# Hashed attention and a two-layer block on one core: other issuers for weight and v loads, engine copies for batch 0's half stacks, a revised planner, and other PSUM tiles for the last output block

## The chip, the cores and the metric

The kernel runs on one core of one Trainium2 chip. The core has a matrix engine (TensorE, PE in the profile, with PEld for its weight loads), a vector engine (VectorE, DVE), a scalar engine (ScalarE, ACT), a general engine (GpSimd, POOL) and a synchronising engine (SyncE, SP) that here only issues DMA transfers. Each engine runs its own instructions strictly in the order in which they stand and waits on semaphores for the others. The metric is the device time of one execution in microseconds (us); less is better.

## The reference

For each of 4 batches and 8 heads, queries and keys get a 6-bit bucket from the signs of a projection; a query sees only the keys of its bucket. Softmax of the scaled scores, times v, gives `attn_out`. Its rows then pass through two matrix products with a squared ReLU between them.

```python
q_bits = (np.einsum('bhsd,dk->bhsk', q, proj) > 0).astype(np.int64)
k_bits = (np.einsum('bhsd,dk->bhsk', k, proj) > 0).astype(np.int64)
mask = q_bucket[:, :, :, None] == k_bucket[:, :, None, :]
scores = np.where(mask, scale * np.matmul(q, k.transpose(0, 1, 3, 2)), -1000000000.0)
...
x = np.ascontiguousarray(attn_out.transpose(0, 2, 1, 3)).reshape(B * S, H * D)
h = np.maximum(x @ w_in, 0.0)
return (h * h @ w_out).astype(np.float32)
```

Sizes: sequence 768, head dimension 64, 3072 tokens, model width 512, hidden width 2048. Everything is float32.

## The kernel before

**Tiling.** The attention is cut into 32 visits: one pair of heads and one half of the sequence (384 queries) each. A visit has six units (three blocks of 128 queries for each head). A unit makes scores of 128 x 768 in PSUM (`pS`, or `pS2` under the name `po` for some early units), VectorE copies them to `e` with the row minimum of the negated scores, ScalarE takes the exponential and its sum, GpSimd or VectorE adds 1e-9 (`rv`), VectorE takes the reciprocal. In the first four visits (`PLAIN_AV`, line 54) GpSimd multiplies `e` by `rv`, TensorE transposes it in float32 (`pT`) and ScalarE or VectorE copies the result to `aT`. In the other 28 visits `e` becomes two fp16 parts (`hl`), which a DMA transposes. `av` then multiplies with v into `pA`, and `xx` takes the result as two fp16 parts.

**Half stacks.** For each head `prep` (lines 631 to 662) loads `R`, 64 rows of transposed keys over 64 rows of transposed queries, splits it into fp16 `A` and the remainder `L`, and builds with five copies of 64 x 768 the operands (`Q`, `A`) and (`M`, `L`) of two score matmuls. The five copies (lines 650 to 652, 659, 660) are DMAs from SBUF to SBUF. Visit 0 is loaded in another form (`first`).

**Weights.** `fetch` (lines 548 to 557) loads 512 columns of raw float64-packed weights (`raw`, three buffers under the tag `hl`); ScalarE or VectorE makes `top`, VectorE makes `f`, then `f` is split into an fp16 high part and the remainder (`win`, `wo`). There are 16 such pieces of w_in and 16 of w_out, nearly all needed early.

**The two-layer block.** When the four head pairs of a batch and half are done, `moe` (lines 807 to 880) runs: for each of 16 slices of the hidden width 12 matmuls into `pm`, ReLU (`g32`), square, split to two fp16 parts `g`, and 9 matmuls into `po`, a PSUM tile of three banks, one for each block of 128 tokens. After the last slice each bank is copied to `o` and sent out. There are eight such blocks, called 0 to 7 here; each is spread among the visits that follow.

**What sets the order.** All operations are first recorded, each with its dependences and one or more ways (engine and instruction). `order` (lines 245 to 272) then plans: `forward` (318 to 399) places operations on engines in simulated time by priorities and by the costs of `cost` (195 to 225), `backward` turns the plan into new priorities, and of five rounds the shortest plan is emitted. An operation with several ways goes to the engine where the plan sees it done first. So a number in the planner can move any instruction. `emit` also puts filler matmuls (`idle<-ones`, line 420) where the plan expects TensorE to wait early on. As every instruction is issued in `emit`, the profile gives nearly all of them the line 427 (424 for grouped matmuls); tiles tell them apart. A second copy of the whole program for inputs out of range follows behind a branch and isn't executed; its instructions are not spoken of.

Of the kernel before, what the change touches and what calls it, by code (L numbers as in the profile page):

```python
# [23 lines left out]
P = 128  # L24
# [105 lines left out]
class Program:  # L130
# [24 lines left out]
    @staticmethod  # L155
    def region(view):
        ap, rec = view.ap, view.rec
        size = lambda dims: 1 + sum(st * (n - 1) for st, n in dims)
        if rec.kind == "dram":
            return 0, 1, ap.offset, ap.offset + size(ap.ap), 0, 0, 0  # L160
        p0, f0 = divmod(ap.offset, rec.row)
        if rec.kind == "psum":
            return 0, 1, f0 // 512, 1 + (f0 % rec.row + size(ap.ap[1:]) - 1) // 512, 0, 0, 0

        (step, n), inner = ap.ap[1], size(ap.ap[2:])
        block = (step, f0 % step, f0 % step + inner) if n > 1 and f0 % step + inner <= step else (0, 0, 0)
        return (p0, p0 + ap.ap[0][1], f0, f0 + size(ap.ap[1:])) + block

    def add(self, *ways):


        ways = [w for w in ways if w[0].key != "pool" or not any(isinstance(x, View) and x.rec.kind == "psum" for x in w[2])]
        queue, name, args, kw = ways[0]
        if name == "matmuls":
            used = [(x, n == 0) for a, _ in args for n, x in enumerate(a)]
        else:
            used = [(args[0], True)] + [(x, False) for x in args[1:]] + [(x, k == "accum_out") for k, x in kw.items()]
        used = [(x.rec, w, self.region(x)) for x, w in used if isinstance(x, View)]
        i, deps = len(self.ops), set()
        for rec, w, (p0, p1, f0, f1, fs, g0, g1) in used:  # L180
            if rec.before is not None:
                deps |= rec.before.ops
            for j, w2, (a0, a1, b0, b1, bs, c0, c1) in rec.accesses:
                if (w or w2 or rec.kind == "psum") and a0 < p1 and p0 < a1 and b0 < f1 and f0 < b1 and not (fs and fs == bs and (c1 <= g0 or g1 <= c0)):
                    deps.add(j)
        for rec, w, r in used:
            rec.ops.add(i)
            rec.accesses.append((i, w, r))
        deps.discard(i)
        if self.mark is not None:  # L190
            self.paced.append((i, self.mark))
        self.ops.append(Op([w + (self.cost(w[0].key, *w[1:]), self.port(w[0].key, *w[1:])) for w in ways], deps, self.rank))

    @staticmethod
    def cost(key, name, args, kw):
# [3 lines left out]
        if name == "matmuls":  # L199

            side = {32: 4, 64: 2}.get(size(args[0][0][1]), 1)
            t = sum(size(a[2]) * column.get(a[2].dtype, 1 / 2.4) + 7 for a, _ in args) / side
            return t, t
        kinds = [x.rec.kind if isinstance(x, View) else "" for x in args]
# [7 lines left out]
        if name.startswith("dma"):  # L212
            b = int(np.prod(args[0].shape)) * mybir.dt.size(args[0].dtype)
            inside = name == "dma_start_transpose" or kinds[:2] == ["sb", "sb"]
            busy = 1040 if key == "pool" else (650 if inside else 475) + 50 * (key == "act")
            return busy, b / (TRANSPOSES if name == "dma_start_transpose" else 314)
        if key == "act":
# [3 lines left out]
        else:  # L221
            fast = name in ("tensor_copy", "tensor_scalar") and "psum" not in kinds[:2]
            both = len(args) > 3 and isinstance(args[3], View) and args[3].shape[-1] == 1
            t = 67 + 100 * ("accum_out" in kw) + n / (1.92 if fast else 0.96) + 62 * (ptr and (fast or name == "scalar_tensor_tensor")) + 100 * both
        return t, t
# [9 lines left out]
    def port(key, name, args, kw):  # L235
# [82 lines left out]
    def forward(self, prio, near):  # L318
# [7 lines left out]
        free = dict.fromkeys(keys, 0.0)  # L326
        out, dma, dge, held, kind = [], 0.0, 0.0, 0.0, None

# [10 lines left out]
        while True:  # L339
# [44 lines left out]
            if o.name.startswith("dma"):  # L384
                dge = max(dge, t) + busy if k != "pool" else dge
                busy = dge - t if k != "pool" else busy
                dma = max(dma, t + busy + (650 if k != "pool" else 450))
                if o.name == "dma_start_transpose":
                    o.busy = busy = dma + 467 - t
                dma += done  # L390
                done = dma + 910 - t
            free[k], o.end = t + busy, t + done
# [56 lines left out]
def run(ctx: ExitStack, tc, kq, v, proj2, w_in, w_out, consts, out, flag):  # L449
# [56 lines left out]
    if fast:  # L506
# [124 lines left out]
    def prep(b, hp):  # L631
# [12 lines left out]
        for odd, R in enumerate(Rs):  # L644
# [4 lines left out]
            pr.rank = r0 + STACKS  # L649
            send(f32(Q[T]), f32(A[U]))  # L650
            send(f32(Q[U]), f32(L[U]))
            send(f32(A[U]), f32(A[T]))
            for half in range(2):
# [4 lines left out]
                dve.tensor_scalar(M[:, w], pc, masks[:, 0:1], masks[:, 1:2], ALU.subtract, ALU.max)  # L658
            send(f32(L[U]), f32(M[T]))
            send(f32(M[T]), f32(Q[T]))  # L660
            out.append(((Q, A), (M, L)))
# [57 lines left out]
    def values(b, hp, plain):  # L719
# [3 lines left out]
        if fast:  # L723
            vscales[b] = VS, None
            RV = sb([P, 2, KC, D], F32, "V", tag="VV" if plain else "R")
            send(RV, v[b, hp])
            if plain:
# [79 lines left out]
    def moe(n, b, half):  # L807
# [6 lines left out]
        for f in range(NF + 1):  # L814
# [23 lines left out]
            if f > 0:  # L838
# [4 lines left out]
                if first:  # L843
                    po = ps([P, 3, DM], F32, "po")
                for t in range(3):
                    gh = g[:, 0, t * P : (t + 1) * P]
                    gl = g[:, 1, t * P : (t + 1) * P]
                    pr.rank, pr.mark = RANK_PE, pace()
                    pe.matmul(po[:, t], gh, wo[:, 0, m], start=first, stop=False)
                    pe.matmul(po[:, t], gh, wo[:, 1, m], start=False, stop=False)  # L850
                    pe.matmul(po[:, t], gl, wo[:, 0, m], start=False, stop=last)
                    pr.mark = None
# [5 lines left out]
                for t in range(3):  # L858
                    r0 = b * S + half * HS + t * P
                    if grouped and last:  # L860
                        if m == 3:
                            move(acc[:, t], po[:, t], back)
                        else:
                            dve.scalar_tensor_tensor(acc[:, t], po[:, t], back, acc[:, t], ALU.mult, ALU.add)
# [168 lines left out]
```

## Time and profile before

| | |
|---|---|
| median of 3 runs | 832.73 us (830.81 to 833.39) |
| the profiled execution | 834.86 us, its span 833.1 us |
| PE busy | 794.3 us, 95% |
| ACT busy | 656.6 us, 79% |
| DVE busy | 605.2 us, 73% |
| POOL busy | 72.7 us, 9% |
| DMA | 145.93 MB, mean 175 GB/s |

The span runs from the first to the last recorded event of the execution; 1.76 us lie around it. Busy times are of the whole span. A row of a group of instructions gives the engine, the operation, the tiles (written and read), the shape, the count, then the total busy time in us and the mean of one in ns, then the idle time in front and who ended it. A row of the list in order of time begins with the start and the length in us, and ends with the idle time before it and its releaser, in brackets.

### The profile page before, as it was taken

Reading aid. Unit: us, or ns where it says so; the run is one execution under the profiler, and the core shown is the slowest. Engines: PE = TensorE matmul, PEld = TensorE weight load, DVE = VectorE, ACT = ScalarE, POOL = GpSimd, SP = SyncE. Lnnn points to the kernel's source line nnn. Section 1 sums busy time; section 2 is a strip of 40 time slices with the busy share of each in tenths; the row PEclk is TensorE's granted clock in tenths of the full one; section 3 lists DMA queues with packets and bytes.
Section 4 is the critical chain, followed back from the end, with each engine's and each line's share of the span. In section 5 each row is a group of like instructions: output and inputs, shape, how many; then the busy total and the mean of one; then the engine's idle time right before and its main releaser. Section 6 shows DMA issues by size and latency. Waiting matters only on the chain. (4 is left out here: it accounts for less than half of the span.)

```text
span 833.1 us, 14383 instructions
## 1 busy us (share of the span) xinstructions
PE 794.3 (95%) x5001; PEld 430.0 (52%) x5001; DVE 605.2 (73%) x1200; ACT 656.6 (79%) x1238; POOL 72.7 (9%) x175
## 2 busy tenths in 40 slices
PE   7797799999999999999999999999999999999996
PEld 4354355555555554555555545555555554555553
DVE  6888989998999888898879755888889433611110
ACT  5898999998888989888898856888988997334443
POOL 1255200100000010000000000000002000000000
PEclk9999999999999999999999999999999999999999
DMA  8985979999999999999989866988975889501001
GB/s 258 270 223 181 292 188 179 214 176 195 183 202 196 195 188 213 192 181 219 194 188 186 212 165 140 181 143 148 146 133 99 239 290 304 212 1 39 1 1 42
DMA packets 299521, 145.93 MB, mean 175 GB/s; under 512 B 268752, under 2 KB 279344, under 8 KB 299440
## 3 DMA queue, kind: packets, MB, share of 16 engines
q1 hardware_dynamic: 299440, 144.93, 77.2%
q8 instruction: 41, 0.67, 0.3%
q14 instruction: 40, 0.33, 0.1%
HBM read 56.80 MB, written 6.29 MB: 76 GB/s over the span
## 5 line engine op out<-in xcount | busy, mean ns | idle before, releaser
L427 PE MATMUL po<-wo,g 128*128 128x512 f16 x1152 | 296.9, 379 | 5.7 <-ACT o L427 5.7
L427 PE MATMUL pm<-xx,win 128*128 128x384 f16 x1536 | 297.7, 326 | 4.4 <-ACT g L427 2.8
L427 PEld LDWEIGHTS <-win 128*128 128x128 f16 x1536 | 149.9, 98 | 116.6 <-issue 8.0
L427 DVE TENSOR_SCALAR_CACHE_REDUCE e<-pS 128x768 f32<-128x768 f32 x192 | 182.7, 953 | 21.9 <-PE pS L427 17.7
L427 ACT ACTIVATE e<-e,maxes 128x768 f32<-128x768 f32 x192 | 178.2, 929 | 20.7 <-DVE e L427 19.2
L427 DVE SCALAR_TENSOR_TENSOR hl<-e,rv,hl 128x768 f16<-128x768 f32 x168 | 171.0, 1019 | 18.8 <-ACT hl L427 17.8
L427 PEld LDWEIGHTS <-g 128*128 128x128 f16 x1152 | 111.9, 98 | 124.8 <-issue 9.1
L427 ACT ACTIVATE hl<-e,rv 128x768 f16<-128x768 f32 x168 | 154.6, 923 | 6.0 <-DMA aT<-hl 5.2
L427 DVE SCALAR_TENSOR_TENSOR g<-g,g 128x384 f16<-128x384 f32 x121 | 66.9, 553 | 111.8 <-ACT g L427 111.4
L427 ACT ACTIVATE g<-g 128x384 f32<-128x384 f32 (+1 forms) x251 | 129.4, 517 | 6.6 <-PE po L427 2.7
L427 ACT ACTIVATE g<-pm 128x384 f32<-128x384 f32 x127 | 61.2, 482 | 90.3 <-PE pm L427 90.0
L427 PE MATMUL pS<-A,Q 128*128 128x384 f16 x372 | 93.1, 330 | 4.1 <-DVE e L427 2.6
L427 PE MATMUL pS<-L,M 128*128 128x384 f16 x372 | 91.8, 327 | 0.8 <-DMA M<-Q 0.8
L424 PE MATMUL pA<-aT,VV 128*64 128x384 f16 x1008 | 87.2, 327 | 0.0
L427 POOL TENSOR_SCALAR rv<-sums 128x1 f32<-128x1 f32 x136 | 36.8, 271 | 541.7 <-ACT e L427 400.2
L424 PEld LDWEIGHTS <-VV 128*64 128x64 f16 x1008 | 54.7, 110 | 32.9 <-issue 10.0
L427 PEld LDWEIGHTS <-Q 128*128 128x128 f16 x372 | 34.2, 98 | 43.1 <-issue 16.2
L427 DVE TENSOR_SCALAR M<-pc,masks 128x384 f16<-128x384 f32 x64 | 43.0, 672 | 15.4 <-PE pc L427 15.2
L427 PEld LDWEIGHTS <-M 128*128 128x128 f16 x372 | 36.3, 98 | 25.1 <-DMA M<-Q 1.2
L427 ACT ACTIVATION_READ_ACCUMULATOR e<-e,maxes 128x1 f32 x192 | 36.6, 191 | 0.0
L427 DVE SCALAR_TENSOR_TENSOR L<-R,A 128x768 f16<-128x768 f32 x32 | 30.4, 950 | 7.7 <-ACT A L427 7.5
L427 PE MATMUL pT<-unit_f,e 128*128 128x128 f32 x144 | 23.8, 293 | 10.5 <-ACT aT L427 7.7
(82 smaller groups left out, 517.4 us busy)
## 6 DMA issues: line engine op xcount, KB each, us to landing
R<-kq SPq DMA_DIRECT2D x32, 384.0 KB, 3.8
X<-kq SPq DMA_DIRECT2D x32, 384.0 KB, 4.1
raw<-w_in SPq DMA_DIRECT2D x16, 511.8 KB, 5.6
raw<-w_out SPq DMA_DIRECT2D x16, 511.8 KB, 4.9
V<-vp SPq DMA_DIRECT2D x20, 384.0 KB, 5.1
out<-o SPq DMA_DIRECT2D x24, 256.0 KB, 2.7
X<-vp SPq DMA_DIRECT2D x16, 384.0 KB, 4.4
Q<-L SPq DMA_DIRECT2D x32, 96.0 KB, 2.9
```

The costliest lines, as they stand in the source:

```text
L424: ins = q.engine.matmul(*map(real, args), **kw).ins
L427: ins = getattr(q.engine, o.name)(*map(real, o.args), **{k: real(x) for k, x in o.kw.items()}).ins
```

## The change

- `HALVES`: in batch 0 (`HALVES_TO` = 1) each of the five half-stack copies may be done by SP (a DMA), GpSimd or VectorE; elsewhere it stays a DMA.
- `RAW_BY`: from the fourth piece on (`RAW_FROM` = 3) a raw weight piece may be loaded by SP or by GpSimd. `V_BY` holds only SP. In the order that results GpSimd issues no transfer at all: all 32 weight pieces and all 20 loads of v stand on SP, as before.
- The planner: a transfer isn't placed while its queue is more than `AT_MOST` (2000 ns) behind; there are two queue clocks that slow each other; a limit of eight SP transfers in flight (`LANES`); other prices for transfers, for two-byte copies on VectorE and for matmuls of 64 rows in pairs; VectorE operations with two inputs no longer count as using the port that VectorE and GpSimd share; a PSUM tile counts as one region.
- The last two-layer block: instead of the three banks of `po`, its outputs are two banks of a `pS` tile and a `pA` tile, and the copy of the middle one is put on VectorE.
- `codes` shares the buffers of `g32`.

```diff
+RAW_BY, V_BY = ("sp", "pool"), ("sp",)
+HALVES, HALVES_TO = (("sp", "pool", "dve"),) * 5, 1
+AT_MOST, RAW_FROM = 2000, 3
...
-        return inside and (len(ins) == 2 or name in ("tensor_copy", "tensor_scalar"))
+        return inside and name in ("tensor_copy", "tensor_scalar")
...
+            if way[1].startswith("dma") and rings[int(k == "pool")] > t + AT_MOST:
+                heapq.heappush(later[k], (rings[int(k == "pool")] - AT_MOST, i))
+                continue
...
-        send(raw.rearrange("p n t -> p (n t)").bitcast(U16)[:, 0:2047], src.bitcast(U16)[:, 1:2048])
+        pr.add(*[(getattr(pr, x), "dma_start", (raw.rearrange("p n t -> p (n t)").bitcast(U16)[:, 0:2047], src.bitcast(U16)[:, 1:2048]), {}) for x in (RAW_BY if turn[0] >= RAW_FROM else ("sp",))])
...
-            send(f32(Q[T]), f32(A[U]))
-            send(f32(Q[U]), f32(L[U]))
-            send(f32(A[U]), f32(A[T]))
+            by = lambda n: tuple(getattr(pr, x) for x in (HALVES[n] if fast and b < HALVES_TO else ("sp",)))
+            move(f32(Q[T]), f32(A[U]), 1.0, by(0))
+            move(f32(Q[U]), f32(L[U]), 1.0, by(1))
+            move(f32(A[U]), f32(A[T]), 1.0, by(2))
...
-                    po = ps([P, 3, DM], F32, "po")
+                    if fast and n == 2 * B - 1:
+                        po = ps([P, 2, 512], F32, "pS"), ps([P, 512], F32, "pA")
+                        po = [po[0][:, 0], po[0][:, 1], po[1]]
+                    else:
+                        po = ps([P, 3, DM], F32, "po")
+                        po = [po[:, t] for t in range(3)]
...
-                        move(o, po[:, t], back)
+                        move(o, po[t], back, (dve,) if fast and t == 1 else (act, dve, pool))
```

Of the 160 half-stack copies 34 leave SP: 21 stand on VectorE and 13 on GpSimd. The order of nearly everything else moves a little too. Three places follow.

SP, near the program's start, behind the constants and the first three weight pieces (`raw`), before:

```order
L427 DMA V_182<-vp 128x768
L427 DMA Q_189<-L_140 64x768
L427 DMA R_195<-kq 128x768
L427 DMA Q_189<-A_97 64x768
L427 DMA R_216<-kq 128x768
L427 DMA Q_221<-L_191 64x768
L427 DMA Q_221<-A_173 64x768
L427 DMA raw_237<-w_in 128x2047
L427 DMA V_241<-vp 128x768
L427 DMA raw_276<-w_out 128x2047
```

The same place now:

```order
L444 DMA R_208<-kq 128x768
L444 DMA R_234<-kq 128x768
L444 DMA unit_f_248<-consts 128x128
L444 DMA raw_252<-w_in 128x2047
L444 DMA raw_266<-w_out 128x2047
L444 DMA raw_301<-w_out 128x2047
L444 DMA V_330<-vp 128x768
L444 DMA Q_307<-A_148 64x768
L444 DMA V_348<-vp 128x768
```

The copies between the loads are gone but for one, the head loads `R` and the weights come ahead of v, and `unit_f` (the identity of the transposes) comes behind them.

GpSimd, its first work, before (`e<-e,rv` is the normalising of one unit's 128 x 768 exponentials, `rv` its small forerunner):

```order
L427 TENSOR_SCALAR rv_257<-sums_244 128x1
L427 TENSOR_SCALAR e_232<-e_232,rv_257 128x768
L427 TENSOR_SCALAR rv_283<-sums_244 128x1
L427 TENSOR_SCALAR e_246<-e_246,rv_283 128x768
L427 TENSOR_SCALAR rv_338<-sums_244 128x1
```

and now:

```order
L444 TENSOR_SCALAR Q_212<-A_140 64x768
L444 TENSOR_TENSOR win_246<-f_239,win_246 128x512
L444 TENSOR_SCALAR rv_264<-sums_259 128x1
L444 TENSOR_SCALAR e_244<-e_244,rv_264 128x768
L444 TENSOR_SCALAR L_144<-M_232 64x768
L444 TENSOR_SCALAR rv_311<-sums_259 128x1
L444 TENSOR_TENSOR win_246<-f_295,win_246 128x512
L444 TENSOR_SCALAR rv_352<-sums_259 128x1
L444 TENSOR_SCALAR Q_359<-L_345 64x768
L444 TENSOR_SCALAR e_261<-e_261,rv_311 128x768
```

Half-stack copies and remainders of weights now stand among the normalisings.

TensorE, its last matmuls, before (`g` are the two fp16 parts of the hidden slice; the three banks of `po` are filled in turn):

```order
L427 MATMUL po_8985<-wo_460,g_9387 128x512
L427 LDWEIGHTS g_9365
L427 MATMUL po_8985<-wo_460,g_9365 128x512 [waits Activation_49]
L427 LDWEIGHTS g_9387
L427 MATMUL po_8985<-wo_460,g_9387 128x512
L427 LDWEIGHTS g_9387
L427 MATMUL po_8985<-wo_460,g_9387 128x512
L427 LDWEIGHTS g_9387
L427 MATMUL po_8985<-wo_460,g_9387 128x512 [waits Activation_49]
```

and now:

```order
L444 LDWEIGHTS g_9391
L444 MATMUL pA_9021<-wo_451,g_9391 128x512
L444 LDWEIGHTS g_9413
L444 MATMUL pS_9007<-wo_451,g_9413 128x512
L444 LDWEIGHTS g_9391
L444 MATMUL pA_9021<-wo_451,g_9391 128x512
L444 LDWEIGHTS g_9391
L444 MATMUL pA_9021<-wo_451,g_9391 128x512
L444 LDWEIGHTS g_9413
L444 MATMUL pA_9021<-wo_451,g_9413 128x512
```

The two waits for ScalarE (its copies of the first two banks) are gone from TensorE's last matmuls.

ScalarE has no single place; counted in its order, this is what stands ahead of its first ReLU of the two-layer block (`g32<-pm`), where the counts differ:

| ScalarE, ahead of the first `g32<-pm` | before | now |
|---|---|---|
| `A<-R` 128x768 | 7 | 8 |
| `VV<-V` 128x768 | 2 | 3 |
| `aT<-pT` 128x384 | 46 | 48 |
| `bits<-pd` 128x384 | 4 | 5 |
| `e<-e,maxes` 128x768, with its sum | 27 | 28 |
| `top<-raw` 128x512 | 24 | 27 |
| `win<-f` and `wo<-f` 128x512 | 23 | 22 |

On VectorE, ahead of its fourth `xx<-pA`, there are 21 half-stack copies, four `f<-raw` and six small `rv` operations more, and two `L<-R`, two `aT<-pT`, one `A<-R`, one `VV<-V` and six remainders of weights fewer. On GpSimd, ahead of the 24th normalising, there are 13 half-stack copies, eight remainders of weights, two `L<-R` and one `wo<-f` more. On TensorE, ahead of the first `pm`, there are 27 fillers, four small `pd` matmuls and three score matmuls more.

More of the change, by code (lines that the diff above doesn't have):

```diff
@@ L64 @@
 RUN = 18
+LANES = 8
 CONSTS_BY, WIDE = ("sp", "sp", "sp"), 1
@@ L162, in region @@
         if rec.kind == "psum":
-            return 0, 1, f0 // 512, 1 + (f0 % rec.row + size(ap.ap[1:]) - 1) // 512, 0, 0, 0
+            return 0, 1, 0, 1, 0, 0, 0
         (step, n), inner = ap.ap[1], size(ap.ap[2:])
@@ L183, in add @@
             for j, w2, (a0, a1, b0, b1, bs, c0, c1) in rec.accesses:
-                if (w or w2 or rec.kind == "psum") and a0 < p1 and p0 < a1 and b0 < f1 and f0 < b1 and not (fs and fs == bs and (c1 <= g0 or g1 <= c0)):
+                if (w or w2) and a0 < p1 and p0 < a1 and b0 < f1 and f0 < b1 and not (fs and fs == bs and (c1 <= g0 or g1 <= c0)):
                     deps.add(j)
@@ L202, in cost @@
             t = sum(size(a[2]) * column.get(a[2].dtype, 1 / 2.4) + 7 for a, _ in args) / side
+            if args[0][0][1].shape[0] == D and len(args) == 2:
+                t *= 0.5 if args[0][0][2].dtype == F32 else 0.7
             return t, t
@@ L215, in cost @@
             busy = 1040 if key == "pool" else (650 if inside else 475) + 50 * (key == "act")
-            return busy, b / (TRANSPOSES if name == "dma_start_transpose" else 314)
+            return busy, SETUP + b / (TRANSPOSES if name == "dma_start_transpose" else INSIDE if inside else LOADING)
         if key == "act":
@@ L223, in cost @@
             both = len(args) > 3 and isinstance(args[3], View) and args[3].shape[-1] == 1
-            t = 67 + 100 * ("accum_out" in kw) + n / (1.92 if fast else 0.96) + 62 * (ptr and (fast or name == "scalar_tensor_tensor")) + 100 * both
+            t = 67 + 100 * ("accum_out" in kw) + n / (3.84 if fast and all(mybir.dt.size(x.dtype) == 2 for x in args[:2]) else 1.92 if fast else 0.96) + 62 * (ptr and (fast or name == "scalar_tensor_tensor")) + 100 * both
         return t, t
@@ L386, in forward @@
                 busy = dge - t if k != "pool" else busy
-                dma = max(dma, t + busy + (650 if k != "pool" else 450))
+                ring = int(k == "pool")
+                dma = max(rings[ring], t + busy + (650 if k != "pool" else 450))
                 if o.name == "dma_start_transpose":
                     o.busy = busy = dma + 467 - t
-                dma += done
-                done = dma + 910 - t
+                shared = min(done, max(0.0, rings[1 - ring] - dma))
+                rings[1 - ring] += shared
+                dma = rings[ring] = dma + done + shared
+                done = dma + LANDING - t
+                if k != "pool":
+                    lanes.append(t + done)
+                    if len(lanes) >= LANES:
+                        busy = max(busy, lanes[-LANES] + 60 - t)
             free[k], o.end = t + busy, t + done
@@ L658, in prep @@
                 dve.tensor_scalar(M[:, w], pc, masks[:, 0:1], masks[:, 1:2], ALU.subtract, ALU.max)
-            send(f32(L[U]), f32(M[T]))
-            send(f32(M[T]), f32(Q[T]))
+            move(f32(L[U]), f32(M[T]), 1.0, by(3))
+            move(f32(M[T]), f32(Q[T]), 1.0, by(4))
             out.append(((Q, A), (M, L)))
@@ L725, in values @@
             RV = sb([P, 2, KC, D], F32, "V", tag="VV" if plain else "R")
-            send(RV, v[b, hp])
+            pr.add(*[(getattr(pr, x), "dma_start", (RV, v[b, hp]), {}) for x in V_BY])
             if plain:
@@ L848, in moe @@
                     pr.rank, pr.mark = RANK_PE, pace()
-                    pe.matmul(po[:, t], gh, wo[:, 0, m], start=first, stop=False)
-                    pe.matmul(po[:, t], gh, wo[:, 1, m], start=False, stop=False)
-                    pe.matmul(po[:, t], gl, wo[:, 0, m], start=False, stop=last)
+                    pe.matmul(po[t], gh, wo[:, 0, m], start=first, stop=False)
+                    pe.matmul(po[t], gh, wo[:, 1, m], start=False, stop=False)
+                    pe.matmul(po[t], gl, wo[:, 0, m], start=False, stop=last)
                     pr.mark = None
@@ L861, in moe @@
                         if m == 3:
-                            move(acc[:, t], po[:, t], back)
+                            move(acc[:, t], po[t], back)
                         else:
-                            dve.scalar_tensor_tensor(acc[:, t], po[:, t], back, acc[:, t], ALU.mult, ALU.add)
+                            dve.scalar_tensor_tensor(acc[:, t], po[t], back, acc[:, t], ALU.mult, ALU.add)
                         if m == NF - 1:
```

7 lines of the change are left out of this document (4 added, 3 removed).

## The prediction

> **What bounds the kernel now.** The totals of each engine on the page come first, then the busy times of each engine by stretch.
>
> ```profile
> PE 794.3 (95%) x5001; PEld 430.0 (52%) x5001; DVE 605.2 (73%) x1200; ACT 656.6 (79%) x1238; POOL 72.7 (9%) x175
> ...
> 0.00:12.00 12.00, 8.78 (x75) 6.03 (x76) 5.20 (x20) 4.30 (x6) 0.21 (x4) 1.00 0.74 229
> 12.00:97.70 85.70, 65.87 (x411) 37.30 (x409) 74.39 (x156) 76.32 (x157) 35.89 (x49) 0.96 0.84 244
> 97.70:140.00 42.30, 40.58 (x243) 21.23 (x243) 38.40 (x78) 41.22 (x77) 3.39 (x8) 1.00 0.85 197
> 140.00:600.00 460.00, 456.74 (x3006) 248.00 (x3004) 392.33 (x793) 393.77 (x716) 25.52 (x99) 1.00 0.92 185
> 600.00:756.00 156.00, 153.41 (x907) 81.79 (x905) 84.85 (x140) 111.58 (x229) 7.74 (x15) 1.00 0.65 174
> 756.00:833.00 77.00, 68.93 (x367) 35.63 (x365) 9.99 (x18) 29.40 (x57) 0.00 (x0) 0.97 0.06 22
> ```
>
> In each row the columns after the length are the busy us of PE, PEld, DVE, ACT and POOL, then clock, DMA share and GB/s. From 97.7 to 756 us TensorE is busy for 650.7 of 658.3 us: there it is the bound, and its work isn't changed (the same matmuls, 27 fillers aside). So time can come or go in three ways: how much TensorE idles before 97.7 (23.0 us of the span), the 7.6 us of gaps up to 756, and the 8.1 us after that. Why 97.7 is the border shows in order of time:
>
> ```profile
> 97.17 0.47 ACT L427 ACTIVATE xx<-pA 128x384 f16<-128x384 f32 x1
> ...
> 97.70 0.32 PE L427 MATMUL pm<-xx,win 128*128 128x384 f16 x1 [1.04 <-ACT xx L427]
> ```
>
> That is the first `pm` of block 0. It is released by ScalarE. Ahead of it stand only attention units, which ScalarE and VectorE feed while they also convert the weights; behind it TensorE always has block work. From 12 us to there ScalarE is busy 76.3 of 85.7 us, VectorE 74.4: **the start is bound by these two**, TensorE waits for them.
>
> **The start, step by step.** `A` is the time of the first `pm`. The order gives ScalarE, ahead of its first ReLU, one `A<-R`, one `VV`, two `aT`, one `bits`, one exponential with its sum and three `top` more, and one weight split less. The rows with their means:
>
> ```profile
> L427 ACT ACTIVATE e<-e,maxes 128x768 f32<-128x768 f32 x192 | 178.2, 929 | 20.7 <-DVE e L427 19.2 <-DVE rv L427 1.2
> L427 ACT ACTIVATION_READ_ACCUMULATOR e<-e,maxes 128x1 f32 x192 | 36.6, 191 | 0.0
> L427 ACT ACTIVATE top<-raw 128x512 f16<-128x512 bf16 x32 | 25.0, 780 | 4.1 <-DMA raw<-w_out 2.2 <-DMA raw<-w_in 1.5
> L427 ACT ACTIVATE A<-R 128x768 f16<-128x768 f32 x30 | 24.9, 834 | 6.8 <-DMA R<-kq 6.8
> L427 ACT ACTIVATE aT<-pT 128x384 f32<-128x384 f32 x46 | 20.7, 484 | 2.6 <-PE pT L427 2.4
> L427 ACT ACTIVATE VV<-V 128x768 f16<-128x768 f32 x15 | 12.5, 834 | 2.3 <-DMA V<-vp 2.3
> L427 ACT ACTIVATE wo<-f 128x512 f16<-128x512 f32 x16 | 9.8, 618 | 0.0
> L427 ACT ACTIVATE bits<-pd,masks 128x384 bf16<-128x384 f32 x16 | 9.2, 576 | 3.5 <-PE pd L424 2.8 <-PE pc L427 0.6
> ```
>
> 0.83 + 0.83 + 2 x 0.48 + 0.58 + 1.12 + 3 x 0.78 - 0.62 = 6.05 us of printed lengths. ScalarE's instructions overlap at their ends:
>
> ```profile
> 57.77 0.82 ACT L427 ACTIVATE top<-raw 128x512 f16<-128x512 bf16 x1
> ...
> 58.41 0.64 ACT L427 ACTIVATE win<-f 128x512 f16<-128x512 f32 x1
> ```
>
> 0.82 us long, but the next starts 0.64 us later. With some 0.15 us less for each of eight more instructions the term is **+4.9 us**. At the idle share of before (9.4 of 85.7 us) it would put `A` 5.5 us later. Against it stand ScalarE's waits for transfers:
>
> ```profile
> ACT A L427 <- DMA R<-kq: 4.6, 2, 3.0
> ...
> ACT top L427 <- DMA raw<-w_out: 2.0, 2, 1.6
> ACT top L427 <- DMA raw<-w_in: 1.5, 3, 0.6
> ```
>
> (This is the list of waits up to 98 us; the columns are total, times, longest.) Without the very first, 3.0 us long, they are 5.1 us. The new order takes 34 copies of 96 KB off SP, and loads of weights and heads come ahead of v there; I take 3 us of the 5.1 as won (0 and 5.1 are the ends), so `A` comes 2.5 us later (0.4 to 5.5).
>
> **The copies.** 21 go to VectorE, 13 to GpSimd. No copy of fp16 to fp16 is in the trace; the nearest rows are:
>
> ```profile
> L427 DVE TENSOR_SCALAR A<-R 128x768 f16<-128x768 f32 x2 | 1.1, 548 | 0.0
> L427 DVE TENSOR_SCALAR rv<-sums 128x1 f32<-128x1 f32 x56 | 8.4, 151 | 6.3 <-ACT e L427 5.4
> L427 POOL TENSOR_SCALAR e<-e,rv 128x768 f32<-128x768 f32 x24 | 24.5, 1028 | 14.9 <-PE pT L427 6.1 <-DVE rv L427 5.9 <-ACT aT L427 2.2
> L427 POOL TENSOR_TENSOR win<-f,win 128x512 f16<-128x512 f32 x3 | 3.5, 1173 | 4.1 <-ACT win L427 4.0
> ```
>
> On VectorE a copy costs between 0.15 (an operation with next to no data) and 0.55 us; I take 0.4, nearer to the row of the same length. So 21 x 0.4 = 8.4 us (3.2 to 11.6), of which the six remainders and the `L`, `aT`, `A` and `VV` that leave VectorE (some 8.5 us, less some 3.7 us for four `f`, six small operations and a `top` that come) give back 4.8: VectorE has +3.6 us ahead of `A` (-1.6 to +6.8). It idled 11.3 us from 12 to 97.7, so this is hidden behind ScalarE's term; without the cover it would be 3.6 us. GpSimd gets 13 x 1.03 + 8 x 1.17 and two `L` and a weight part, together some 25 us ahead of the 24th normalising. It was busy 35.9 us of 85.7; now about 61. I cost that at 0 in the forecast, since GpSimd still idles 25 us; the first rival has it otherwise.
>
> TensorE does more before `A`: four `pd` (half of a row of eight) and three score matmuls.
>
> ```profile
> 23.95 0.85 PE L424 MATMUL pd<-R,pj 128*32 128x384 f32 x8
> ...
> 98.13 0.48 PE L427 MATMUL pS<-A,Q 128*128 128x384 f16 x2
> 98.46 0.32 PE L427 MATMUL pS<-L,M 128*128 128x384 f16 x1
> ```
>
> Each of the four `pd` of the order is two such matmuls, so 0.85, and two score matmuls take 0.33 us to the next: 0.5. That is **-1.3 us** (work already done is not lost). From 97.7 to 140 TensorE idled 1.7 us, beside a ScalarE busy 41.2 of 42.3; there ScalarE now has about 8 us less to do up to the ninth ReLU (3 less by then in printed lengths, after 6 more at the first), so I take -0.5 of the 1.7. The 27 fillers at 0.09 us each (next row) lie in idle time of TensorE before 97.7; were it not idle there, they would cost 2.5 us.
>
> ```profile
> L420 PE MATMUL idle<-ones 128*128 128x128 bf16 x67 | 6.2, 265 | 3.0 <-DVE ones L427 3.0
> ```
>
> **Start: +2.5 - 1.3 - 0.5 = +0.7 us** (-2.6 to +4.2, or to 6.7 with the fillers).
>
> **The middle.** 140 to 756 us has 5.9 us of gaps; the order is reshuffled, no engine gets more work. I take 0 (-2 to +2).
>
> **The end.** The last block before, in order of time:
>
> ```profile
> 763.17 0.60 ACT L427 ACTIVATE o<-po 128x512 f32<-128x512 f32 x1 [0.16 <-PE po L427]
> ...
> 763.82 1.02 PE L427 MATMUL po<-wo,g 128*128 128x512 f16 x4 [0.69 <-ACT o L427]
> ...
> 824.25 0.60 ACT L427 ACTIVATE o<-po 128x512 f32<-128x512 f32 x1 [1.64 <-PE po L427]
> ...
> 824.90 0.81 PE L427 MATMUL po<-wo,g 128*128 128x512 f16 x3 [0.69 <-ACT o L427]
> 825.74 0.60 ACT L427 ACTIVATE o<-po 128x512 f32<-128x512 f32 x1 [0.90 <-PE po L427]
> 826.39 0.59 PE L427 MATMUL po<-wo,g 128*128 128x512 f16 x2 [0.69 <-ACT o L427]
> ...
> 827.02 0.60 ACT L427 ACTIVATE o<-po 128x512 f32<-128x512 f32 x1 [0.68 <-PE po L427]
> ```
>
> Thrice TensorE stands 0.69 us because a bank of the same tile is being read. With `pS` and `pA` block 7 needn't wait for block 6's reads, and the last matmuls into `pA` run beside the copies from `pS`. All three waits go: **-2.1 us**. What is late next is the last copy from `pA` on ScalarE, 0.6 us as before, and its transfer. VectorE's copy of the middle bank waits for ScalarE's copy of the first, and both end about when `pA` is full; the ends are -0.7 (if the pair delays the last transfer) and -2.1.
>
> **Sum.** +0.7 + 0 - 2.1 = -1.4 us on the profiled execution's 834.86 us (its span 833.1 and 1.76 around it), so 833.5. That execution lay 2.1 us above the median of 832.73; against the median the forecast is **831.3 us**, its own range 828.5 to 834.2.
>
> **The rivals.** *GpSimd holds up the start.* Each of the 24 normalisings now stands behind copies and remainders in GpSimd's queue, and TensorE's transposes wait for it. Busy 61 of 85.7 us, GpSimd is in another operation 0.7 of the time when an `e` is ready, with half of 1.17 us to go: 24 x 0.4 = 10 us, half of it covered by the second unit that runs beside. Start +5.7, sum +3.6: **836.3**. For it: GpSimd and VectorE do delay each other:
>
> ```profile
> 25.57 1.44 POOL L427 TENSOR_SCALAR e<-e,rv 128x768 f32<-128x768 f32 x1 [0.99 <-DVE rv L427]
> 25.63 0.69 DVE L427 SCALAR_TENSOR_TENSOR f<-raw,top 128x512 uint32<-128x512 uint32 x1 [0.16 <-ACT top L427]
> ```
>
> An `e`, 1.03 us in the mean, took 1.44 beside VectorE's `f`, and the new planner no longer counts such two-input operations. Against it: even then GpSimd idles a quarter of the stretch. It decides slower if the first `pm` starts after about 104 us (2.5 + 2.1 + 1.3 + 0.5 us later). The Trainium skill ("SBUF — State Buffer", Who interferes with whom) has the port pair of the two engines locked for a whole instruction, also by a VectorE operation with two SBUF inputs; by that rule 23 more GpSimd operations of up to 0.69 us of blocking would cost them up to 16 us, which speaks for this rival. The row at 25.57 agrees with it.
>
> *The start gets faster.* SP's queue, free of copies that waited for their sources, brings weights and heads in time, and ScalarE's idle time from 12 us on falls from 9.4 to 3 us: `A` -1.5, with the -1.3 and -1.2 of the stalls behind it -4.0; sum -6.1: **826.6**. For it: the DMA share of 0.84 up to 97.7. Against it: the 4.9 us.
>
> *Nothing but noise.* GpSimd issues no transfer, so that part of the change doesn't do what it says and costs nothing; if the end too wins only 0.7 and the start loses 0.7, **832.7**.
>
> **How the numbers follow.** Forecast 0.48 (0.18 of it faster by over 0.3%, 2.5 us, about what a measurement of this kernel can tell from no change; 0.30 within), faster start 0.24 (all faster), GpSimd 0.21 (0.20 slower), nothing 0.07 (within). Together faster 0.42, same 0.38, slower 0.20. The range takes in 826.6 and 836.3 with the ends of the copies and of the fillers: **825 to 838 us**.
>
> **What would show it.** The first `pm` at 100 us, with ScalarE busy over 80 us before it; a first `pm` before 97 or after 104 shows a rival. The operations on `e` wait for GpSimd now as follows (total us, times):
>
> ```profile
>   POOL e L427: 11.1, 11
> ```
>
> Much more than that, or normalisings with a mean over 1.2 us, show GpSimd's. No wait of `po` on `o` in the last block, and the last matmul about 2 us nearer to the end of block 6, show the end. More than 8 us of TensorE gaps from 140 to 756 would prove the middle wrong.

## The result: 853.37 us, and the profile after

| | before | after |
|---|---|---|
| median | 832.75 us (830.81 to 833.39, 4 runs) | 853.37 us (852.57 to 855.88, 4 runs) |
| ratio, 95% interval | | 1.0257 [1.0228, 1.0285] |
| the profiled execution | 834.86 us | 852.69 us, its span 850.8 us |

The changed kernel is 20.6 us slower. The forecast was 831.3 us with a range up to 838, so size and sign were both missed. Where the 17.7 us of span went is read from the same view as in the prediction, the busy times by stretch. First the page's totals of TensorE after, its 40 slices and the clock:

```profile
PE 804.3 (95%) x5028; PEld 433.2 (51%) x5028; DVE 622.5 (73%) x1215; ACT 655.7 (77%) x1232; POOL 111.5 (13%) x200
...
PE   8777789999999996999999999999999999999996
...
PEclk9899999999999996999999999999999999999999
```

There is a dip in the sixteenth slice, in TensorE's busy share and in its clock, that the page of before doesn't have. The stretches of after (length, then busy us of PE, PEld, DVE, ACT, POOL, then clock, DMA share, GB/s):

```profile
0.00:140.00 140.00, 109.28 (x668) 59.94 (x669) 121.62 (x244) 113.17 (x218) 75.39 (x88) 0.96 0.68 195
140.00:300.00 160.00, 159.73 (x1072) 87.71 (x1070) 139.39 (x284) 138.25 (x254) 12.86 (x36) 1.00 0.93 177
300.00:345.00 45.00, 37.34 (x222) 18.54 (x220) 36.04 (x76) 33.44 (x59) 1.64 (x6) 0.85 0.93 192
345.00:600.00 255.00, 254.66 (x1660) 137.55 (x1659) 203.91 (x403) 210.34 (x381) 14.03 (x52) 1.00 0.86 176
600.00:756.00 156.00, 155.29 (x925) 83.43 (x923) 90.99 (x161) 120.43 (x244) 7.56 (x19) 1.00 0.66 157
756.00:850.80 94.80, 88.04 (x490) 46.01 (x488) 30.56 (x50) 40.10 (x80) 0.00 (x0) 0.98 0.28 94
```

and the two of before that they are to be held against:

```profile
0.00:140.00 140.00, 115.22 (x727) 64.56 (x728) 118.00 (x252) 121.84 (x238) 39.48 (x61) 0.98 0.83 229
...
300.00:345.00 45.00, 43.85 (x284) 23.51 (x283) 39.36 (x83) 40.13 (x75) 3.43 (x9) 1.00 0.96 201
```

TensorE's idle time grows by 7.7 us (850.8 - 804.3 against 833.1 - 794.3): 5.9 more up to 140, 6.5 more from 300 to 345, 3.4 less in the rest of the middle, 1.4 less at the end. Its busy time grows by 10.0 us with the same work: 1.9 are the 27 further fillers (6.2 to 8.1 us in their group), the other 8.1 are the same matmuls taking longer, for a large part at a lower clock (worked out behind the steps below). So there are **two places of loss, the start and a hole at 300 to 345 us**.

**The start.** The first `pm` stands at 110.62 us instead of 97.70. The stretch up to it, in the columns above:

```profile
12.00:110.60 98.60, 73.62 (x444) 39.42 (x441) 91.06 (x177) 83.19 (x166) 69.93 (x74) 0.95 0.66 198
```

VectorE is now busy for 91.1 of 98.6 us (before 74.4 of 85.7), GpSimd for 69.9 (35.9). Groups up to the first `pm` of after, VectorE and GpSimd:

```profile
L444 DVE SCALAR_TENSOR_TENSOR f<-raw,top 128x512 uint32<-128x512 uint32 x26 | 24.8, 958 | 0.2 <-issue 0.2
...
L444 DVE TENSOR_SCALAR Q<-A 64x768 f16<-64x768 f16 x4 | 3.1, 773 | 0.1
...
L444 DVE TENSOR_SCALAR A<-A 64x768 f16<-64x768 f16 x6 | 2.2, 359 | 0.1
...
L444 POOL TENSOR_SCALAR e<-e,rv 128x768 f32<-128x768 f32 x24 | 28.4, 1189 | 8.8 <-DVE rv L444 6.7 <-PE pT L444 1.4
L444 POOL TENSOR_TENSOR win<-f,win 128x512 f16<-128x512 f32 x9 | 12.1, 1351 | 8.9 <-ACT win L444 8.7
L444 POOL TENSOR_SCALAR L<-M 64x768 f16<-64x768 f16 x5 | 5.9, 1182 | 0.7 <-DVE M L444 0.3
```

Up to its own first `pm`, the kernel before had this row for the same operation `f`:

```profile
L427 DVE SCALAR_TENSOR_TENSOR f<-raw,top 128x512 uint32<-128x512 uint32 x22 | 15.3, 698 | 0.9 <-ACT top L427 0.9
```

VectorE spends 9.5 us more on `f`, of which four more of them are 2.8; the other 6.7 come from all 26 taking 0.26 us longer each, beside a busy GpSimd. The 21 copies cost another 10.8 us. Who waits shows in the list of waits up to 110.6 us (total, times, longest):

```profile
PEld pT L444 <- POOL e L444: 14.3, 13, 2.3
...
PE pT L444 <- POOL e L444: 6.0, 4, 1.6
...
SPq L444 <- DVE f L444: 36.9, 16, 6.7
```

SP's queue, which the copies were to leave free, now waits three times as long as before (12.5 us up to 98) for VectorE to read `raw`, whose three buffers the next weight loads need. DMA is less busy (0.66 against 0.84). That these later loads cost time isn't shown: from 12 us to the first `pm` ScalarE waits for no transfer.

**The hole.** TensorE in order of time, after:

```profile
317.52 0.49 PE L444 MATMUL pS<-L,M 128*128 128x384 f16 x2
...
319.06 0.48 PE L444 MATMUL pS<-A,Q 128*128 128x384 f16 x2 [0.89 <-DVE e L444]
...
321.92 0.80 PE L444 MATMUL pS<-A,Q 128*128 128x384 f16 x2 [1.89 <-DVE e L444]
...
324.41 0.80 PE L444 MATMUL pS<-A,Q 128*128 128x384 f16 x2 [0.74 <-DVE e L444]
...
326.91 0.80 PE L444 MATMUL pS<-A,Q 128*128 128x384 f16 x2 [1.06 <-DVE e L444]
...
332.62 4.23 PE L441 MATMUL pA<-aT,VV 128*64 128x384 f16 x36
```

There are no `pm` and no `po` here: attention stands alone, and its units come every 2.5 us (324.41, 326.91), as fast as VectorE frees `pS`. From 321.9 the same pair of matmuls takes 0.80 instead of 0.48 us. In the order this stretch of TensorE's work without a block matmul is 10.9 us long by printed lengths; in the trace it lasts 23.3 us, from 314.2 to the `pm` at 337.46. Before, the longest such stretch after the first 100 us is 5.1 us, and elsewhere (at 171 us). Ahead of the hole TensorE has done all 384 `pm` and all 288 output matmuls of blocks 0 and 1: the plan uses them up before block 2 can begin.

### The profile page after: what moved, and what is told of

Its sections match the earlier page's. It is cut to its first block, busy times and chain, and to the rows that moved or that the text cites. A ratio compares the mean times of both kernels' runs of the same rounds, so it can differ in the third digit from the quotient of the medians.

```text
span 850.8 us, 14371 instructions
## 1 busy us (share of the span) xinstructions
PE 804.3 (95%) x5028; PEld 433.2 (51%) x5028; DVE 622.5 (73%) x1215; ACT 655.7 (77%) x1232; POOL 111.5 (13%) x200
## 4 chain that ended last, share of the span: by engine, by line
PE 79%; DVE 9%; ACT 4%; issue 4%; POOL 2%; DMA 0%; SPq 0%; DVEq 0%; POOLq 0%; ACTq 0%
PE pm L444 26%; PE po L444 24%; PE pS L444 14%; PE pA L441 9%; DVE f L444 2%; DVE e L444 2%; ACT e L444 1%; PE pA L444 1%; PE pd L441 1%; PE pc L444 1%; DVE hl L444 1%; POOL win L444 1%; PE pS L441 1%; ACT g L444 1%; PE idle L437 1%
## 5 line engine op out<-in xcount | busy, mean ns | idle before, releaser
L444 PE MATMUL pm<-xx,win 128*128 128x384 f16 x1536 | 308.0, 326 | 3.5 <-ACT g L444 1.8
L444 PE MATMUL po<-wo,g 128*128 128x512 f16 x1008 | 279.4, 379 | 1.4 <-ACT o L444 0.6
L444 ACT ACTIVATE g<-pm 128x384 f32<-128x384 f32 x128 | 62.1, 485 | 98.3 <-PE pm L444 97.7
L444 ACT ACTIVATE g<-g 128x384 f16<-128x384 f32 (+1 forms) x253 | 130.6, 516 | 6.3 <-PE po L444 2.5
L444 PE MATMUL pS<-A,Q 128*128 128x384 f16 x372 | 95.7, 332 | 13.9 <-DVE e L444 13.8
L444 POOL TENSOR_SCALAR rv<-sums 128x1 f32<-128x1 f32 x128 | 33.9, 265 | 506.7 <-ACT e L444 317.7
L444 PE MATMUL pS<-L,M 128*128 128x384 f16 x372 | 96.1, 331 | 0.4 <-DVE M L444 0.4
L444 PE MATMUL pS<-wo,g 128*128 128x512 f16 x96 | 34.9, 379 | 0.0
```

What stands on the lines that cost most here:

```text
L444: ins = getattr(q.engine, o.name)(*map(real, o.args), **{k: real(x) for k, x in o.kw.items()}).ins
```

## The experiments

Five kernels (1 and 4 to 7) keep a plan as it is and replace instructions in place; the others are planned anew with a number changed. Every run has the kernel before beside it on the same chip (832.5 to 832.7 us).

**1. The copies back to SP, nothing else moved** (changed kernel, after the planning):

```diff
+        for o in self.ops:
+            if len(o.ways) > 1 and any(w[1] == "dma_start" for w in o.ways) and o.args[0].shape[0] == D and o.queue is not self.sp:
+                o.queue, o.name, o.args, o.kw = next(w for w in o.ways if w[0] is self.sp)[:4]
```

> The changed kernel's plan is kept instruction by instruction; only its 34 engine copies of half stacks are made DMAs on SyncE again, at the same place in the order. Theory C (the copies on VectorE and GpSimd hold up the start): first pm at 100 to 103 us instead of 110.6, total 842 to 846 us. Theory W (the weight work on GpSimd holds it up) or theory Q (ScalarE's longer list does): first pm stays at 108 to 112 us, total 850 to 855. On every theory the low clock between some 300 and 340 us stays.

Measured: 864.91 us, ratio 1.0388 [1.0364, 1.0411]; the first `pm` at 121.3. TensorE waits for the copies now:

```profile
PE pS L447 <- DMA M<-Q: 18.8, 4, 6.9
```

No theory gave this number. At the places that this order gives them, copies on SP's queue come still later than on the engines. So the price of the copies can't be read by sending them back in place: the order was made around them. The next two are planned anew.

**2. No copies on engines, planned anew:**

```diff
-HALVES, HALVES_TO = (("sp", "pool", "dve"),) * 5, 1
+HALVES, HALVES_TO = (("sp", "pool", "dve"),) * 5, 0
```

> The changed kernel planned anew with HALVES_TO = 0, so no half stack is copied by an engine. ScalarE has 94.4 us of printed lengths ahead of its first ReLU instead of 105.7, GpSimd 36 instead of 58 ahead of the 24th normalising; the stretch of attention alone before block 2 stays in the order. Theories C, W and Q all say: first pm at 95 to 100 us. Theory H (the stretch of attention alone costs 8 to 11 us): total 839 to 844. If the stretch costs nothing: 829 to 834.

Measured: 843.54 us, 1.0127 [1.0109, 1.0145]. The first `pm` is back at 94.7 us, the hole stays:

```profile
300.00:345.00 45.00, 37.82 (x229) 18.70 (x228) 36.50 (x73) 36.41 (x63) 3.83 (x11) 0.92 0.99 205
```

**3. The planner's old prices of transfers, copies kept:**

```diff
-TRANSPOSES, INSIDE, LOADING = 165, 230, 325
-SETUP, LANDING = 100, 1350
+TRANSPOSES, INSIDE, LOADING = 165, 314, 314
+SETUP, LANDING = 0, 910
```

> The changed kernel planned anew with the old prices of transfers (314 bytes per ns, no SETUP, landing 910); the order has no stretch of attention alone before block 2, while the copies stay on the engines. Theory H: no low clock and no gap between 140 and 700 us, total 840 to 846, with the first pm still at 105 to 111. If the clock falls by itself, whatever the order: a low clock again, total 850 to 856.

Measured: 841.53 us, 1.011 [1.0088, 1.0132]. The first `pm` stays late, at 107.4, and the hole is gone:

```profile
300.00:345.00 45.00, 44.39 (x312) 23.97 (x310) 39.58 (x82) 39.88 (x74) 4.69 (x11) 1.00 0.95 194
```

**4. The end alone** (kernel before, its order kept; the last block's `po` becomes a pair of `pS` and `pA`):

```diff
...
+                    if fast and n == 2 * B - 1:
+                        po.rec.make = lambda: Split(psp.tile([P, 2, 512], F32, name="pS", tag="pS", bufs=1), psp.tile([P, 512], F32, name="pA", tag="pA", bufs=1))
```

> The kernel before with its plan kept, but the last block's outputs in a pS and a pA tile instead of po. All three waits of 0.69 us go: 830.0 to 831.5 us, 2.1 faster at most, and 0.7 faster if the last transfer is put off. The rival that the end gives nothing: 832.7.

Measured: 832.42 us, 0.9998 [0.9984, 1.0012]. The last `o` ends at 824.26 us, 7.1 us ahead of the span's end; before, it ended at 827.62, 5.5 ahead. Of the three waits one is gone, one is 0.47 long, and the one of 0.69 within block 6's end stays; by this one profile what is gained is lost again behind the last copy. The order is that of before, yet the first `pm` stands at 94.8 instead of 97.7: the start of one order alone differs by some 3 us between executions.

**5. GpSimd's weight work to VectorE** (changed kernel, order kept):

```diff
+        for o in self.ops:
+            if o.queue is self.pool and len(o.ways) > 1 and o.args[0].shape[1:] == [512] or o.queue is self.pool and len(o.ways) > 1 and tuple(o.args[0].shape) == (P, 512):
+                o.queue, o.name, o.args, o.kw = next(w for w in o.ways if w[0] is self.dve)[:4]
```

> The changed kernel with its order kept; what GpSimd does to the weights (all 512-wide remainders and halves of win and wo) goes to VectorE at the places where it stands. GpSimd then has some 28 us less before the first `pm`, VectorE some 19 us more (about 24 parts at 0.7 to 0.8). Theory G (the start came later because normalisings stand behind 1.2 to 1.6 us operations in GpSimd's queue): the waits for `e` on POOL go down to under 12 us, the first `pm` comes at 100 to 106 instead of 110.6, the time is 843 to 850. Theory V (VectorE and GpSimd lock each other out, and VectorE, busy 92% of the stretch, is the bound): with still more on VectorE the first `pm` comes at 113 to 122, the time is 856 to 866. The slow stretch from 305 to 340 us stays by both.

Measured: 856.39 us, 1.0282 [1.0262, 1.0301]; first `pm` at 114.2. The waits for GpSimd fall, and it is slower all the same:

```profile
PEld pT L447 <- POOL e L447: 9.5, 10, 2.2
```

Theory V's numbers came. In the changed kernel the start is not held up by GpSimd's queue alone; VectorE, busy for 95.7 of the 102.2 us from 12 us on, holds it up too.

**6 and 7. The copies alone, in the order of before,** all 40 on VectorE, then all 40 on GpSimd:

```diff
...
+        for o in self.ops:
+            if o.name == "dma_start" and o.half:
+                o.queue, o.name, o.args = self.dve, "tensor_scalar", (o.args[0], o.args[1], 1.0, 1.0, ALU.mult, ALU.mult)
...
```

(`half` marks batch 0's half-stack copies; in 7 `self.pool` stands for `self.dve`.)

> The kernel before with its order kept; only the 40 copies of halves of batch 0 go from SP's transfers to VectorE, at the same places of the order. By the durations in the trace of after (0.36 to 0.78 us) they cost VectorE 40 x 0.55 = 22 us, against 11.3 us of idle time before the first `pm`, less those few that lie behind it. Theory V (VectorE's work is what counts): first `pm` at 105 to 112 instead of 95 to 98, time 840 to 848. Theory O (the copies themselves are hidden or pay for themselves by SP's relief; the loss is the order that the planner made with them): first `pm` at 94 to 100, time 829 to 836.

> As the run before with its 40 copies, but on GpSimd: 40 x 1.2 us = 48 us, GpSimd busy 84 of 86 us if all lay before the first `pm`. Theory G (GpSimd's queue holds up the normalisings): first `pm` at 108 to 125, time 843 to 860, waits for `e` on POOL over 25 us. Theory O (only the order counts): first `pm` at 94 to 100 and 829 to 836. Theory V: between, 98 to 104 and 833 to 840, as VectorE is only slowed by the port.

Measured: 846.13 us, 1.0165 [1.0146, 1.0185], and 849.73 us, 1.0214 [1.0189, 1.0239]; the first `pm` at 108.2 and 112.1. Groups of experiment 6 up to its first `pm`:

```profile
L435 DVE SCALAR_TENSOR_TENSOR f<-raw,top 128x512 uint32<-128x512 uint32 x22 | 15.0, 685 | 0.1
...
L435 DVE TENSOR_SCALAR A<-A 64x768 f16<-64x768 f16 x8 | 4.8, 604 | 0.2
```

The stretch from 12 us to that `pm` in 6:

```profile
12.00:108.20 96.20, 72.17 (x414) 39.22 (x412) 93.70 (x195) 77.88 (x157) 39.01 (x49) 0.91 0.54 176
```

and what waits in SP's queue in 6:

```profile
SPq L435 <- DVE f L435: 55.7, 18, 11.0
```

VectorE is full (93.7 of 96.2 us), and the loads wait 55.7 us for it, though ScalarE waits for no transfer from 12 us on. The 40 copies cost it 19.7 us in their five groups, 0.49 each. The waits for `e` grow here too, although GpSimd got no more to do:

```profile
PEld pT L435 <- POOL e L435: 12.4, 9, 3.1
PE pT L435 <- POOL e L435: 6.9, 6, 2.3
```

Together that is 19.3 us, nearly the 20.3 of the changed kernel. So these waits alone don't tell GpSimd's queue from a late VectorE, which feeds it `rv` (GpSimd's own waits for that are 18.7 us here, 5.9 before). Groups of experiment 7:

```profile
L435 DVE SCALAR_TENSOR_TENSOR f<-raw,top 128x512 uint32<-128x512 uint32 x22 | 19.0, 868 | 0.0
...
L435 POOL TENSOR_SCALAR Q<-A 64x768 f16<-64x768 f16 x8 | 8.3, 1038 | 2.8 <-ACT A L435 2.2
```

its waits:

```profile
PEld pT L435 <- POOL e L435: 24.0, 13, 3.7
...
PE pT L435 <- POOL e L435: 15.3, 8, 3.3
```

and the stretch up to its first `pm`:

```profile
12.00:112.10 100.10, 72.00 (x409) 39.18 (x409) 81.48 (x158) 78.11 (x156) 75.57 (x87) 0.90 0.53 170
```

Here VectorE does no copy and is still slower: `f` takes 0.87 instead of 0.70 us (0.69 in 6, where GpSimd got nothing more). It is not full, though (81.5 of 100.1 us); GpSimd, busy 75.6, delays the normalisings. The Trainium skill ("SBUF — State Buffer", Who interferes with whom) says that a VectorE operation with two SBUF inputs and a GpSimd operation that reads SBUF hold each other up; this row agrees. Theories V (for 6) and G (for 7) hold; theory O, that the copies are hidden, falls in both. Without any change of the order the copies cost 13.6 and 17.2 us.

**8. Both causes undone** (no copies on engines and old prices, the rest of the change kept):

```diff
-TRANSPOSES, INSIDE, LOADING = 165, 230, 325
-SETUP, LANDING = 100, 1350
+TRANSPOSES, INSIDE, LOADING = 165, 314, 314
+SETUP, LANDING = 0, 910
...
-HALVES, HALVES_TO = (("sp", "pool", "dve"),) * 5, 1
+HALVES, HALVES_TO = (("sp", "pool", "dve"),) * 5, 0
```

> The changed kernel, planned anew with two of its parts undone: no halves of batch 0 on engines, and the transfers' old prices (314 bytes per ns, 910 ns to land). Theory S+H (two causes that add: the copies with what the planner does around them hold up the start by some 9 us, and the new transfer prices let it use up blocks 0 and 1 too early, which leaves a stretch of attention alone at 305 us, another 9): first `pm` at 93 to 98, no stretch with the clock under 0.9 between 300 and 345 us, time 829 to 835. Theory 1 (one cause seen twice: each part undone alone already gave all there is): 839 to 843 as each alone. What is left of the change then (v and weights by their queues, the limit on queued transfers, the last block's tiles) is worth 0 +- 3 by the first theory.

Measured: 829.4 us, 0.9964 [0.9947, 0.998]: faster than both kernels. The first `pm` stands at 97.4, and TensorE is full where the hole was:

```profile
12.00:97.00 85.00, 73.45 (x460) 39.11 (x458) 77.93 (x160) 77.04 (x158) 51.14 (x58) 0.96 0.87 253
...
300.00:345.00 45.00, 44.22 (x287) 23.87 (x286) 41.74 (x86) 40.23 (x75) 1.53 (x8) 1.00 0.98 189
```

The four kernels 2, 3, 8 and the changed one form a square:

| us | old prices | new prices |
|---|---|---|
| no copies on engines | 829.40 | 843.54 |
| copies on engines | 841.53 | 853.37 |

The copies cost 12.1 us with the old prices and 9.8 with the new, the prices 14.1 without copies and 11.8 with them. The two add nearly; neither explains the other. Each number rests on one order for its setting.

**9. As 8, without the limit on queued transfers:**

```diff
-AT_MOST, RAW_FROM = 2000, 3
+AT_MOST, RAW_FROM = 10**9, 3
```

> e8_both planned without the limit on queued transfers (2000 ns becomes without end). The planner then puts more work of ScalarE and VectorE ahead of the first block: 103.9 us of printed lengths on ScalarE before the first ReLU against 97.6 in e8_both, and 97 on VectorE against 90. Theory A (what the two engines have to do ahead of the first block sets the start): first `pm` at 101 to 105 instead of 97.4, time 832 to 837 (+3 to +8). Theory Q (the limit works by how deep SP's queue is, and the list ahead of the first ReLU doesn't matter): within 2 us of e8_both's 829.4.

Measured: 837.11 us, 1.0051 [1.0033, 1.0068], first `pm` at 105.5, each just past the end of theory A's range. The limit is worth some 7.7 us in this setting, by keeping work of ScalarE and VectorE out of the time ahead of the first block.

**10. As 8, raw weights by SP alone:**

```diff
-RAW_BY, V_BY = ("sp", "pool"), ("sp",)
+RAW_BY, V_BY = ("sp",), ("sp",)
```

> e8_both, but raw weights by SP alone as in the kernel before. In e8_both GpSimd issues one of the 32 raw loads; in the changed kernel it issued none. Theory N (that part of the change brings nothing here): 827 to 832, first `pm` at 94 to 99. Theory P (a second queue helps the start): 832 to 836, first `pm` after 100.

Measured: 830.59 us (828.34 to 836.53), 0.9988 [0.9967, 1.001], first `pm` at 94.2. Theory N: this part brings nothing that can be measured here. In the changed kernel it did nothing at all, since GpSimd issued no transfer.

**11. As 8, the last block in `po` again:**

```diff
-                    if fast and n == 2 * B - 1:
+                    if False:
...
-                        move(o, po[t], back, (dve,) if fast and t == 1 else (act, dve, pool))
+                        move(o, po[t], back, (act, dve, pool))
```

> e8_both with the last block's output in one tile `po` again, as before. The prediction had the new tiles worth 2.1 us (three waits of 0.69), the frozen test of them alone gave 0. By the prediction's step: 831 to 833 and three waits of 0.69 in the last block; by the frozen test: 828 to 831 (the last transfers take what TensorE gains).

Measured: 831.33 us, 0.998 [0.9967, 0.9993], inconclusive as a time: it is in the first range and 0.3 us above the second, and the first `pm`, at 100.0, is 2.6 us later than in 8. But the three waits of 0.69 are not there: from 745 us on TensorE waits for no engine. The last matmuls and copies in the order of time:

```profile
818.25 4.26 PE L444 MATMUL po<-wo,g 128*128 128x512 f16 x19
...
822.55 1.57 ACT L444 ACTIVATE o<-po 128x512 f32<-128x512 f32 x3 [2.50 <-PE po L444]
```

With a PSUM tile counted as one region, the planner lets all matmuls into `po` go ahead of its copies, so the old tile has no waits either.

**12. A smaller dose of the hole** (as 8, but 100 ns more for each transfer in the planner):

```diff
-SETUP, LANDING = 0, 910
+SETUP, LANDING = 100, 910
```

> A smaller dose of the hole at 305 us: e8_both with 100 ns more for each transfer in the planner, and nothing else. In its order the longest stretch of attention alone on TensorE between block matmuls is 6.7 us, at the place where the changed kernel has 10.9 and e8_both under 4.2. Theory H (the hole's price follows the length of that stretch, 12 to 14 us for 10.9): some 3 to 7 us of TensorE idle or at a low clock between 300 and 345 us, time 831 to 837 with the first `pm` at 94 to 98. Rival: only the engines' work ahead of the first `pm` counts, and the order's place is harmless: 827 to 830, as ScalarE has 1.5 us less ahead of it than in e8_both.

Measured: 843.05 us, 1.0128 [1.0102, 1.0155]; first `pm` at 98.1. The stretches up to 140 us and of the hole:

```profile
0.00:140.00 140.00, 119.17 (x731) 66.37 (x731) 121.30 (x248) 117.05 (x229) 52.98 (x68) 0.94 0.79 226
300.00:345.00 45.00, 37.29 (x233) 18.42 (x230) 35.47 (x70) 34.06 (x60) 2.10 (x11) 0.92 0.95 189
```

The hole is there, as theory H has it, but the time is 6 us above H's range. Two things were missed. The hole's idle time is as long at 6.7 us of printed work as at 10.9 (7.7 us of 45 in both). And the start does 3.2 us less of TensorE's work by 140 us than in 8 (119.17 against 122.33), though the first `pm` comes only 0.7 us later; its mean clock up to there is 0.94, that of 8 0.98. In time the 100 ns alone cost as much as all the new prices (843.54 us in experiment 2). So the length of the stretch tells that there is a hole, not its price.

## Why the prediction was wrong, step by step

- **What bounds the kernel** held. The start is set by ScalarE and VectorE, and from the first `pm` on TensorE is the bound, but for the hole.
- **ScalarE's work, +4.9 us:** right in sign, 2.0 us too small. From 12 us to the first `pm` it is busy 83.2 us, 6.9 more.
- **ScalarE's waits, -3 us:** this step failed. Its idle time there grew from 9.4 to 15.4 us, 6.0 more; 6.9 and 6.0 are the 12.9 us by which the first `pm` is late (+2.5 forecast). The waits for transfers did go (after 12 us none is left). Waits for VectorE and for TensorE's transposes came in their place:

```profile
ACT e L444 <- DVE e L444: 4.6, 8, 1.0
ACT aT L444 <- PE pT L444: 3.0, 4, 1.4
ACT win L444 <- DVE f L444: 2.7, 2, 1.6
```

- **The copies on VectorE, +3.6 us hidden in 11.3 us of idle time:** this is the mis-sized term at the root. VectorE is busy 16.7 us more by the first `pm`. The copies took 10.8 instead of 8.4 us (0.36 to 0.78 each, past the upper end of 0.55), and the step let the other operations keep their lengths, although `f` took 0.96 instead of 0.70. By experiment 7 GpSimd's added work lengthens `f`. Experiment 6 shows the cover gone: 19.7 us of copies against 11.3 us of idle time.
- **GpSimd's 25 us at a cost of 0** failed too. Its `e` waits rose from 11.1 to 20.3 us. The first rival named this mechanism and its sign for it ("after about 104 us"), but priced it at 5 us, and for GpSimd's queue alone. The `e` waits alone don't show its queue as the cause (experiment 6); experiment 7 does show that work added to GpSimd is not free. By 6 and 7 filling either engine alone is enough to delay the start, and by 5 moving work from GpSimd to VectorE doesn't help. In time the start lost some 10 to 12 us (the square), not +0.7.
- **TensorE's work ahead, -1.3, and the stalls, -0.5:** not to be seen beside this. By 140 us TensorE has been busy 5.9 us less, 1.9 more of that on fillers.
- **The middle, 0 "since no engine gets more work":** failed. The sum of an engine's work says nothing of where it stands. The order, known ahead of the run, already had the stretch without block matmuls; the prediction looked only at the start and the end of it. The sign of being wrong that was named ahead was met: the gaps from 140 to 756 us add up to 9.0 us, 7.7 of them in the hole, with a low clock besides. The new prices of transfers, which the list of the change names and the prediction gave no term, cost 12 to 14 us (the square); the hole's share is 6.5 us of added idle time and, by the estimate below, some 4.5 us of low clock.
- **The end, -2.1 us:** the waits went (none on TensorE in the last block), and its idle time after 756 us fell by 1.4 us. By experiment 4 that isn't worth a measurable time: a part is lost again between the last copy and the end (7.1 us there instead of 5.5). One of the three waits, at 763 us, was also read wrongly: it lies within block 6's own end, where its second group of matmuls waits for the first one's copy.
- **Raw weights and v:** that GpSimd issues none and the part does nothing was right; experiment 10 adds that it is worth nothing when one load is issued there.

- **The range of the forecast alone** (828.5 to 834.2) is narrower than its own terms: their ends add up to -6.7 and +5.5 us, 826.0 to 838.2. The measured time lies far above both.

What the low clock cost can be estimated. These are the stretches at a clock of 0.50, after and then before:

```profile
24.31:31.14 6.83, 6.83 (x25) 2.45 (x24) 5.86 (x11) 4.65 (x10) 4.46 (x6) 0.50 0.71 228
92.58:95.99 3.41, 3.27 (x14) 2.63 (x15) 3.41 (x6) 3.32 (x9) 1.35 (x2) 0.50 0.60 197
321.27:334.93 13.66, 9.10 (x35) 3.75 (x36) 9.80 (x22) 8.44 (x14) 0.77 (x4) 0.50 0.92 199
...
30.41:33.82 3.41, 3.11 (x12) 2.15 (x13) 1.03 (x2) 1.94 (x6) 1.10 (x2) 0.50 0.82 223
64.54:67.96 3.42, 3.30 (x15) 2.24 (x14) 2.62 (x6) 2.81 (x7) 1.35 (x2) 0.50 0.74 266
```

If work takes twice as long at half the clock, half of TensorE's busy time there is lost: 9.6 us after, 3.2 before. By this estimate the lower clock makes up 6.4 of the 8.1 us by which the same matmuls took longer. Some 1.7 us stay open. And experiment 8 rests on one order. Its neighbours 10 and 11 lie at 0.999 and 0.998, so of the 0.36% a part may be the luck of that order.

## What to carry to other kernels

A copy moved from a DMA queue to an engine isn't hidden when the engine is as full in that stage as VectorE was here (74.4 of 85.7 us), and work moved to a second engine can lengthen the first one's (`f` 0.87 instead of 0.70 us in experiment 7). When a planner's prices change, look through the whole new order for stretches in which the bounding engine has only work that waits for another. And test two suspected causes in a square (each undone alone, and both): the sums show whether they are one or two.

## What the runs showed of the hardware

The granted clock of TensorE fell without a long pause. In the hole of the changed kernel no single idle gap is above 1.9 us, and yet the clock went down to 0.50 at 321.27 us and stayed there for 13.7 us (the row is shown above). In the 3.41 us ahead of the fall TensorE was busy for 1.28:

```profile
317.86:321.27 3.41, 1.28 (x7) 0.56 (x6) 3.23 (x6) 1.80 (x3) 0.83 (x1) 1.00 1.01 177
```

The fourteen traces agree: stretches at half the clock last 3.41 us or a multiple of it. Of the 40 falls between 20 us and the last matmul each came after 3.41 us in which TensorE was busy for 8 to 53% of the time. Of the 3199 such stretches at full clock that no fall followed, none was below 43%. (Two falls ahead of 20 us came after 70 and 72%.) What fits is a busy share under about a half in 3.41 us; why some shares between 43 and 53% brought a fall and others none stays open.

A run of 36 `pA` matmuls took 4.23 us at its end, and 3.12 at 314 us. The Trainium skill ("TensorE: Matmul & The Clock Gate", Why this matters for your kernels) advises against gaps above some 3 us between bursts; by that rule these gaps were harmless. Here the measurement decides: two gaps of 0.89 and 1.89 us close behind each other were followed by the half clock.

Copies of 64 x 768 in fp16 took 0.36 to 0.78 us on VectorE and 0.8 to 1.6 us on GpSimd in the changed kernel, as means of their groups. What sets them apart is not shown.
